# Causal scores in nine rounds for four groups instead of ten, and the order of all steps as a written list

## The chip, the cores and the metric

The kernel runs on one core of a Trainium2 chip. Its time is device microseconds of one execution; the median of three runs of the kernel before is 550.99 us (550.4 to 551.45). A profiled execution shows what each engine did: TensorE (PE: matmuls; PEld: its weight loads), VectorE (DVE), ScalarE (ACT), GpSimd (POOL), SyncE (SP, which issues most DMAs). Times in a profile count from the first instruction.

## The reference

Two layers, each an attention block A and a feed-forward block B, with residuals. There are 2048 tokens of width 640. A has 32 heads of 20; the tokens are cut into four segments of 512. Within a segment there is causal softmax attention; across segments a running memory M, z is read and then updated. The two results are mixed by a gate per head.

```python
q, k, v = heads(x @ wq), heads(x @ wk), heads(x @ wv)     # (32, 4 segments, 512, 20)
for s in range(4):
    p = softmax(q[s] @ k[s].T * 20 ** -0.5 + causal)       # 512 x 512 for each head
    a_dot = p @ v[s]
    a_mem = (phi(q[s]) @ M) / (phi(q[s]) @ z + 1e-6)       # phi(t) = t + 1 if t > 0 else exp(t)
    o[s] = sigmoid(beta) * a_mem + (1 - sigmoid(beta)) * a_dot
    M, z = M + phi(k[s]).T @ v[s], z + sum(phi(k[s]))
x = x + merge(o) @ wo
x = x + relu(layernorm(x) @ w1) @ w2                       # 640 -> 1728 -> 640
```

The input of A is layernorm(x) too. All of it is done twice with the same weights.

## The kernel before

One core keeps all weights and x in its memory. The eight pairs of layer and segment go through projections, scores, memory, output projection and feed-forward, and the phases of neighbouring segments overlap.

*Groups, pairs, rounds.* A group is four heads of one segment; there are 64 groups in the two layers, taken in 32 pairs (index m; z is 0 or 1 within a pair). Queries and keys of a pair lie in a padded buffer `pad`, four heads at partitions 0, 32, 64 and 96, twenty rows each; there are four such buffers, filled by SP's DMAs from a scratch tensor in device memory (`fill`). Keys are cut into four blocks j of 128. For block j only queries from 128j on are computed: 512, 384, 256 and 128 columns. `ROUNDS` packs these, for two groups, into five rounds of 512 columns: (z=0, j=0); (z=0, j=1 and 3); (j=2 of both); (z=1, j=0); (z=1, j=1 and 3). A round is issued by `scores` (matmuls at L1301). The four heads of a round use four tiles of 32 by 128 of the array side by side. It writes two slots X and Y of two PSUM banks each, and both must be free.

*Exponentials, masks, apply.* `exps` (L1365) empties each slot with one ScalarE instruction of 128 lanes by 1024 elements into the probability buffer `PT`, of which there is one for z=0 and one for z=1. `causal` (L1377) sets what lies over the diagonal to zero with GpSimd, four masks a group. `apply` (L1397) multiplies the probabilities of a group with its values: 16 matmuls on four tiles of 128 by 32, one for each head; the result lies in one of four single PSUM banks `MISC`, and is evicted to `otu` (L1407). Groups 6 and 7 of the first segment go another way (L1436).

*Everything else.* Projections, feed-forward, memory and transposes (helper lines L774 and L777) also write the four `MISC` banks. L774 issues a matmul on the whole 128 by 128 array, L777 the same work as four matmuls on tiles of 128 by 32. Which form is taken is chosen when a step is placed (`either`). PSUM is evicted by ScalarE or VectorE (`evac`).

*What sets the order.* Each phase is a generator that yields steps with the tokens they wait for. `Sched.run` places one step at a time: of the steps that are ready to be placed it takes the one with the earliest start by its own estimates, corrected by priorities, by allowances for late inputs (`SOFT`, `SOFT_DMA`, `LONE_NS`, `COLS_LAG`), and by a table `SHIFT` of offsets. The result is one fixed instruction sequence for each engine, with semaphores between them; nothing is decided on the chip.

Of the kernel before, what the change touches and what calls it, by code (L numbers as in the profile page):

```python
# [5 lines left out]
dt = mybir.dt  # L6
# [27 lines left out]
PTH = 1280  # L34
BY_TOKEN = range(6,8)
PT_OFF = [0, 512, 1024, 896]
# [73 lines left out]
class Op:  # L110

    def __init__(self, alts, waits, dma=None, acq=None, urgent=False, take=(), mode="full", lag=0.0, port=False):
        self.lag = lag
# [8 lines left out]
        self.urgent = urgent  # L125
        self.take = take
        self.data = 0.0
# [32 lines left out]
class Spawn:  # L160
    def __init__(self, prio, gen):
        self.prio = prio
        self.gen = gen


LONE_NS = 300.0
SWITCH_NS = 96.0
COLS_LAG = 1500.0
SOFT = 400
SOFT_DMA = 1000  # L170
SOFT_FROM = ("sc",6,4,1)
SEM_NS = 60.0
PE_MARGIN = 80.0
HOLDERS = 1
SHIFT = {
# [41 lines left out]
}  # L217
HOLD_TOL = {"pe": 220.0, "act": 150.0, "dve": 200.0, "pool": 0.0, "sp": 0.0}


class Sched:


    def __init__(self, prog):
        self.P = prog
        self.free = {e: 800.0 for e in ENGS}
        self.t = {}
        self.events = {}
        self.streams = []
        self.dma_free = 0.0  # L230
        self.rank = {}
        self.mode = "full"
        self.soon = 0.0
        self.landed = set()
        self.met = {}
        self.seen = {}
        self.phase = {}
        self.made = {}
        self.held = {"dve": [], "pool": []}

    def add(self, prio, gen):
        self.streams.append([prio, gen, None, None, False])
        self.rank[id(gen)] = 0
# [8 lines left out]
    def enter(self, gen, phase):  # L252
        if self.phase.get(id(gen)) != phase:
            self.phase[id(gen)] = phase
            self.made[id(gen)] = 0

    def place(self, n, gen):
        k = self.made.get(id(gen), 0)
        return n, self.phase.get(id(gen), 0), sum(k >= x for x in (6, 20, 60))

# [6 lines left out]
    def _fill(self, st):  # L267
        while st[2] is None and not st[4]:
            try:
                y = next(st[1]) if st[3] is None else st[1].send(st[3][0])  # L270
            except StopIteration:
                st[4] = True
                return
            st[3] = None
            st[2] = y

    def _settle(self, st):

        while True:
            self._fill(st)  # L280
            if st[4]:
                return False
            y = st[2]
            if isinstance(y, (Op, Either)):
                return True
            if isinstance(y, Spawn):
                self.add(y.prio, y.gen)
                self.rank[id(y.gen)] = self.rank[id(st[1])]
                st[2], st[3] = None, (None,)
            elif isinstance(y, Need):  # L290
                if y.key not in self.events:
                    return False
                st[2], st[3] = None, (self.events[y.key],)
            else:
                s = self._pick(y.slots)
                if s is None:
                    return False
                s.free = False
                st[2], st[3] = None, (s,)
# [5 lines left out]
    def _mode(self, op):  # L305
        if op.cols is None:
            return op.mode
# [1437 lines left out]
```

## Time and profile before

| | value |
|---|---|
| median of the runs | 550.99 us |
| profiled execution, first to last instruction | 549.3 us |
| TensorE busy | 539.8 us, 98% |
| VectorE busy | 427.8 us, 78% |
| ScalarE busy | 406.0 us, 74% |
| GpSimd busy | 195.7 us, 36% |
| exponentials L1365 | 320, 308.9 us |
| score matmuls L1301 | 1024 |

"Busy" is the union of the instructions' times. Matmuls are pipelined: one of 512 columns lasts 379 ns in the rows, though the next can start long before that. The time that a matmul takes from the stream is therefore read from start to start in the timeline. A row of a group has the line, the engine, the operation, output and input, the shape, the count, then busy time and mean nanoseconds of one, then the idle time ahead of it and what ended that. A row of the timeline has the start, the length, the engine, the line and the count of merged instructions. In a row of stretches stand the bounds, the length, then busy time for PE, PEld, DVE, ACT and POOL, the granted clock, the DMA share and GB/s.

### The profile page before, as it was taken

How to read it: one execution, taken by the hardware profiler on the slowest of the kernel's cores; microseconds unless marked ns; L12 is line 12 of the kernel's file. 1: busy time of each engine (PE TensorE's matmuls, PEld its weight loads, DVE VectorE, ACT ScalarE, POOL GpSimd, SP SyncE). 2: the span in 40 equal slices, each digit the busy share in tenths (PEclk: the TensorE clock that was granted, in tenths of full speed). 3: DMA queues.
4: the chain of work that ended last, by engine and by line, in shares of the span. 5: the costliest groups of instructions: out<-in, count | busy, mean ns of one | idle time of the engine just before them, and what ended most of it. 6: DMA issues, size and time to landing. Idle time of an engine off the chain costs nothing.

```text
span 549.3 us, 20483 instructions
## 1 busy us (share of the span) xinstructions
PE 539.8 (98%) x9025; PEld 305.5 (56%) x9025; DVE 427.8 (78%) x1067; ACT 406.0 (74%) x516; POOL 195.7 (36%) x305
## 2 busy tenths in 40 slices
PE   7999999999999999999999999999999999999997
PEld 6543464455554546646556555564646654757656
DVE  4899999898999989898778858997899788417102
ACT  5699899789888987788888867897778787350130
POOL 5255444333453334443433423433333333201000
PEclk9999999999999999999999999999999999999999
DMA  8699979715384175438384743336246511541201
GB/s 270 165 198 253 245 158 223 221 44 116 89 165 98 40 180 77 75 68 120 47 212 93 116 116 93 58 69 104 50 139 130 117 32 22 106 63 33 71 2 51
DMA packets 133325, 62.20 MB, mean 113 GB/s; under 512 B 112116, under 2 KB 123124, under 8 KB 133236
## 3 DMA queue, kind: packets, MB, share of 16 engines
q1 hardware_dynamic: 132672, 60.36, 51.5%
q8 instruction: 71, 1.16, 0.9%
q10 hardware_dynamic: 564, 0.53, 0.4%
q14 instruction: 18, 0.15, 0.1%
HBM read 20.56 MB, written 12.85 MB: 61 GB/s over the span
## 4 chain that ended last, share of the span: by engine, by line
PE 88%; ACT 6%; DVE 2%; DMA 2%; SPq 1%; issue 0%
PE ps L774 35%; PE ps L777 35%; PE ps L1301 8%; PE ps L1397 6%; ACT PT L1365 5%; PE ps L1180 2%; DMA x_sb<-in_A_x_dram 1%; PE ps L1572 1%; PE ps L1238 1%; DMA pad<-scr 1%; SPq L602 1%; DVE xn_tok L841 0%; SPq L612 0%; DVE stats L795 0%; DVE x_sb L1614 0%; DVE o_sb L1491 0%
## 5 line engine op out<-in xcount | busy, mean ns | idle before, releaser
L1365 ACT ACTIVATE PT<-ps 128x1024 bf16<-128x1024 f32 x320 | 308.9, 1028 | 59.3 <-PE ps L1301 57.6
L1377 POOL TENSOR_SCALAR_AFFINE_SELECT PT<-PT 128x512 bf16<-128x512 bf16 x256 | 169.3, 679 | 241.1 <-ACT PT L1365 241.0
L777 PE MATMUL ps<-xnT,w_r 128*32 128x512 bf16 x1256 | 76.0, 379 | 0.0
L777 PE MATMUL ps<-w_r,hT 128*32 128x320 bf16 (+1 forms) x1764 | 67.8, 295 | 0.0
L1614 DVE TENSOR_TENSOR x_sb<-x_sb,ps 128x320 bf16<-128x320 bf16 (+1 forms) x65 | 30.7, 474 | 43.6 <-PE ps L777 38.7
L1301 PE MATMUL ps<-pad 20*128 20x512 bf16 (+3 forms) x1024 | 63.4, 301 | 1.2 <-ACT PT L1365 0.7
L774 PE MATMUL ps<-w_r,hT 128*128 128x320 bf16 x404 | 64.2, 300 | 0.0
L795 DVE BATCH_NORM_STATS2 stats<-x_sb 128x6 f32<-128x320 bf16 x124 | 55.0, 478 | 3.8 <-DMA x_sb<-in_A_x_dram 3.0
L777 PEld LDWEIGHTS ps<-w_r,hT 128*32 128x32 bf16 x1764 | 45.2, 97 | 12.6 <-issue 1.4
L1595 ACT ACTIVATE hT<-ps 128x512 bf16<-128x512 f32 x50 | 29.9, 599 | 29.0 <-PE ps L777 25.6
L774 PE MATMUL ps<-xnT,w_r 128*128 128x512 bf16 x206 | 50.8, 380 | 0.0
L774 PEld LDWEIGHTS ps<-w_r,hT 128*128 128x128 bf16 x404 | 37.6, 98 | 19.4 <-issue 4.9
L1301 PEld LDWEIGHTS ps<-pad 20*128 20x128 bf16 x1024 | 17.9, 92 | 52.9 <-issue 24.5
L777 PEld LDWEIGHTS ps<-xnT,w_r 128*32 128x32 bf16 x1256 | 31.6, 97 | 27.8 <-issue 2.0
L1519 DVE TENSOR_TENSOR x_sb<-x_sb,ps 128x320 bf16<-128x320 bf16 x64 | 29.7, 478 | 20.4 <-PE ps L777 16.0
L811 POOL TENSOR_TENSOR rstd<-lnU,mhalf 128x2 f32<-128x2 f32 (+2 forms) x27 | 21.1, 782 | 63.5 <-DVE lnU L807 60.4
L1407 DVE CAST otu<-ps 128x512 bf16<-128x512 f32 x52 | 35.6, 685 | 9.1 <-PE ps L1397 8.2
L1397 PE MATMUL ps<-PT,v_aug 128*21 128x128 bf16 (+3 forms) x896 | 40.3, 300 | 0.0
L1594 DVE TENSOR_SCALAR hT<-ps 128x512 bf16<-128x512 f32 x54 | 36.5, 681 | 1.7 <-PE ps L774 0.7
L1491 DVE TENSOR_TENSOR o_sb<-otk,rden 128x320 bf16<-128x320 bf16 x62 | 34.8, 588 | 0.5
L981 DVE CAST stg<-ps 128x512 bf16<-128x512 f32 (+1 forms) x37 | 24.7, 669 | 12.5 <-PE ps L774 6.3
L1146 ACT ACTIVATE stg<-stg 128x512 bf16<-128x512 bf16 x50 | 31.7, 635 | 2.0 <-DVE rtmp L1144 1.8
(118 smaller groups left out, 731.5 us busy)
## 6 DMA issues: line engine op xcount, KB each, us to landing
pad<-scr SPq DMA_DIRECT2D x124, 80.0 KB
scr<-stg SPq DMA_DIRECT2D x34, 256.0 KB, 2.5
out_dram<-x_sb SPq DMA_DIRECT2D x15, 160.0 KB, 1.9
w_r<-in_B_w_dram SPq DMA_DIRECT2D x10, 216.0 KB, 4.0
w_r<-in_B_w_dram SPq DMA_DIRECT2D x13, 160.0 KB, 2.8
x_sb<-in_A_x_dram SPq DMA_DIRECT2D x10, 160.0 KB, 3.2
scr<-w_r SPq DMA_DIRECT2D x5, 256.0 KB, 4.2
wv_r<-in_A_wv_dram SPq DMA_DIRECT2D x1, 800.0 KB, 9.7
```

What stands on the lines that cost most here:

```text
L774: return e.matmul(view(dst.ap, b), a, b, start=(k == 0), stop=(k == last))
L777: return e.matmul(view(dst.ap[rows], b), part, b, start=(k == 0), stop=(k == last))
L795: tk = yield dve(320, 1, lambda e, c2=c2: e.bn_stats(stats6[:, t, c2, :], x_sb[:, t, c2 * 320:(c2 + 1) * 320]), xt)
L1146: te = yield act(512, lambda e, q=q: e.activation(q, q, ACT.Exp), [tr] + p, psum=False)
L1301: fns.append([(lambda e, z=z, j=j, hh=hh, N=N, o=o, sl=sl, q=hh % 2: e.matmul(slot.ap[:, q, o:o + N], sl.ap[32 * hh:32 * hh + DH, z, 0, 12 ...
L1365: tx = yield act(1024, lambda e, dst=dst, src=src: e.activation(dst, src, ACT.Exp, scale=SCALE), sc + pw)
L1377: tm = yield pool(600.0, lambda e, reg=reg: e.affine_select(out=reg, in_=reg, pattern=[[0, 4], [1, 128]], compare_op=ALU.is_ge, fill=0.0, ...
L1397: fns.append((lambda e, OD, j=j, hh=hh: e.matmul(OD.ap[32 * hh:32 * hh + DH + 1, 128 * j:L], VAUG[vx(a, s)][:, j, 4 * g + hh, :], pt.ap[:, ...
L1407: te = yield evac(L, 1, lambda e: e.tensor_copy(dst, OD.ap), lambda e: e.activation(dst, OD.ap, ACT.Copy), [tk] + OTU[0].tks)
L1491: to = yield dve(320, 1, lambda e, z=z, dst=dst: e.tensor_tensor(dst, av[:, z, :, :, 0:DH], rd.ap[:, z].to_broadcast([128, NJ, 4, DH]), AL ...
L1594: th = yield evac(512, 1, lambda e: e.tensor_scalar(hT[:, dc, :], bk.ap[:, :], 0.0, None, ALU.max), lambda e: e.activation(hT[:, dc, :], b ...
L1614: ta = yield dve(n, 1, lambda e: e.tensor_tensor(x_sb[:, t, c0:c0 + n], x_sb[:, t, c0:c0 + n], bk.ap[:, 0:n], ALU.add), [tk], urgent=True)
```

## The change

*Scores.* For a layer's first segment (`plain(m)`) the five rounds stay. In the other three segments a group's blocks are cut along the diagonal. What is left of the full blocks, without one square of 64 by 64 for each key block, fills two rounds of 512 columns for each group (`FULLS`: 448+64, and 192+256+64 columns). The squares left out, four for each of four heads in four groups (two pairs), make one further round (`DIAG`): 64 matmuls of 64 columns on eight tiles of 32 by 64 of the array, which write lanes 0 to 63 and 64 to 127 separately. It stands behind the second round of every second pair and reads the padded buffers of both pairs. So four groups take nine rounds instead of ten.

*Behind it.* The squares go to a new buffer `DG`, the rest to a shorter `PT` (1024 columns instead of 1280 for a head). A slot of the diagonal round is emptied by two ScalarE instructions of 64 lanes by 1024 elements. The masks are four a group as before, in other places: two on `PT`, both behind the second of its two rounds, and two on `DG`. `apply` takes nine pieces a head instead of four in these segments: 36 matmuls. At the start of these segments in each layer VectorE zeroes a part of `DG`. There are three padded buffers instead of four.

*Tokens.* In every second tile of 128 tokens the two halves of 64 are exchanged in memory, so that the squares of odd key blocks lie in the upper lanes; x is loaded, and the result stored, by DMAs of 64 partitions and two tiles. The last tile's store is split into halves on the queues of SP and ScalarE.

*Order.* The rules, priorities, allowances and the table are gone. A list `ORDER` names, step by step, which generator gives the next step (its number in the order of `S.add`; 40 more for one that it spawned; 80 more for the second form: VectorE instead of ScalarE for an eviction, quarter-width tiles instead of full ones for a matmul group). There are 7192 quarter-width matmuls of L777's kind instead of 4604, and 712 full ones of L774's kind instead of 1359. TensorE changes its tile shape 308 times instead of 322. ScalarE gets 17 more instructions; VectorE has 17 copies fewer.

```diff
-PTH = 1280
+PTH = 1024
-PT_OFF = [0, 512, 1024, 896]
+PT_OFF = [0, 512, None, 896]
+FULLS = (((0, 64, 448), (3, 384, 64)), ((2, 320, 192), (1, 256, 256), (1, 128, 64)))
+DIAG = ((0, 0, 0), (0, 3, 448), (1, 2, 256), (1, 1, 192))
+SUMS = ((0, 0, 448, 64), (3, 448, 64, 384), (2, 512, 192, 320), (1, 704, 256, 256), (1, 960, 64, 128))
-SOFT = 400
-SOFT_DMA = 1000
-SHIFT = {
...
+ORDER = """
+36 37 35 21 36 37*3 36*2 35 21 36 21*2 37 21 26 21*2 22 35 37 26*4 21 22*3 21*2 108 28*3 37 26 23 28 23 148 28 37*6
...
+    def run(self):
+        for word in ORDER.split():
+            code, _, count = word.partition("*")
+            for _ in range(int(count or 1)):
+                n, other = int(code) % 80, int(code) >= 80
+                st = tops[n] if n < 40 else next(x for x in self.kids[id(tops[n - 40])] if not x[3])
+                self._record(st, st[1].fn() if isinstance(st[1], Either) else st[1], other)
...
-        NPAD, NXT, NXN, NPT = 4, 2, 2, 2
+        NPAD, NXT, NXN, NPT = 3, 2, 2, 2
+        DG = sb("DG", [128, 2, 4, 4 * 128])
...
+        def plain(m):
+            return m % (NSEG * G // 2) < G // 2
+        def rounds(m):
+            return [u for u in range(5) if plain(m) or u != 2 or m % 2 == 0]
+        def turn_of(m, u):
+            if plain(m):
+                return [(z, 0, 128 * j, 128, 128 * j, L - 128 * j, o) for z, j, o in ROUNDS[u]]
+            if u == 2:
+                return [(z, 64 * (j % 2), q0, 64, q0, 64, 128 * z + 64 * y) for z in range(4) for y, j, q0 in DIAG]
...
-                        slot.ap[:, q, o:o + N], sl.ap[32 * hh:32 * hh + DH, z, 0, 128 * j:128 * j + 128],
-                        sl.ap[32 * hh:32 * hh + DH, z, 1, 128 * j:L]),
+                        slot.ap[p:p + nk, q, o:o + nq], sl.ap[32 * hh:32 * hh + DH, z, 0, k0:k0 + nk],
+                        sl.ap[32 * hh:32 * hh + DH, z, 1, q0:q0 + nq]),
...
+                            moves = [(DG[r, t].rearrange("p z (h x) -> p h z x", h=4)[:, hs],
+                                      bkp.ap[r].rearrange("p h (z x) -> p h z x", z=4)) for t, r in enumerate(SIDES)]
...
+                sums = [(j, lambda hh, c0=c0, nq=nq: pt.ap[:, hh, c0:c0 + nq], q0, nq) for j, c0, nq, q0 in SUMS]
+                sums += [(j, lambda hh, j=j, y=y: DG[:, j % 2, n % 4, 128 * hh + 64 * y:128 * hh + 64 * y + 64], q0, 64)
+                         for y, j, q0 in DIAG]
```

More of the change, by code (lines that the diff above doesn't have):

```diff
@@ L110, with __init__ @@
 class Op:
-    def __init__(self, alts, waits, dma=None, acq=None, urgent=False, take=(), mode="full", lag=0.0, port=False):
-        self.lag = lag
+    def __init__(self, alts, waits, dma=None, acq=None, take=(), mode="full", port=False):
         self.port = port
@@ L454, in pe, with _times @@
-def pe(ns, fns, waits=(), acq=None, take=(), mode="full", lag=0.0):
-    return Op([("pe", ns, fns, 190.0)], waits, acq=acq, take=take, mode=mode, lag=lag)
+    def _times(self, op, k, waits):
+        e, hold, fns, tail = op.alts[k]
+        m = PE_MARGIN if e == "pe" else 0.0
+        if e == "pe" and op.mode == "cols" and op.cols_ns is not None:
+            hold = op.cols_ns
+        if e == "pe" and op.mode != self.mode:
+            hold = hold + SWITCH_NS
+        start = max([self.at(t) + SEM_NS + m for t in waits], default=0.0)
+        start = max(self.free[e], start)
+        if e == "dve" and op.port:
+            for a, b in self.held["pool"][-6:]:
+                if a <= start + 66.0 < b:
+                    hold = max(hold, b - start + op.data - 70.0)
+        if e == "pool":
+            for a, b in self.held["dve"][-6:]:
+                if a < start + hold and b > start:
+                    hold = hold + b - max(a, start)
+        return start, start + hold
@@ new lines, in run @@
+    def run(self):
+        tops = list(self.streams)
+        first = tops[0]
+        self._settle_all()
+        for word in ORDER.split():
[4 more added lines that the diff above has]
+                self._record(st, st[1].fn() if isinstance(st[1], Either) else st[1], other)
+                self._settle(st)
+                self._settle_all()
+                if isinstance(first[1], Either):
+                    first[1].fn()
+        assert not self.streams
@@ new lines, in _record @@
+    def _record(self, st, op, other):
+        k = int(other and len(op.alts) > 1)
+        e, _, fns, tail = op.alts[k]
+        if op.cols is not None:
+            op.mode = "cols" if other else "full"
+            fns = op.cols if other else fns
+        waits, slot = op.waits, None
+        for s in op.take:
+            s.free = False
+        if op.acq is not None:
+            slot = self._pick(op.acq)
+            slot.free = False
+            waits = waits + slot.tks
+            fns = [(lambda eng, fn=fn, slot=slot: fn(eng, slot), mark) for fn, mark in fns]
+        start, end = self._times(op, k, waits)
+        self.P.waits(e, waits)
+        self.free[e] = end
+        if e == "pe":
+            self.mode = op.mode
+        if e == "dve" and op.port:
+            self.held[e].append((end - op.data, end))
+        elif e == "pool":
+            self.held[e].append((start, end))
+        if op.dma is not None:
+            tk = self.P.dma(e, fns[0][0], op.dma)
+            self.dma_free = max(self.dma_free, start + 300.0) + tail[1]
+            self.t[(id(tk[0]), tk[1])] = max(self.dma_free, end) + tail[0]
+            if tail[2]:
+                self.free[e] = max(end, self.dma_free)
+            out = tk
+        else:
+            marks = []
+            for fn, mark in fns:
+                tk = self.P.op(e, fn, mark)
+                if tk is not None:
+                    self.t[(id(tk[0]), tk[1])] = end + tail
+                    marks.append(tk)
+            out = marks[0] if len(marks) == 1 else (marks or None)
+        st[1], st[2] = None, ((slot, out) if slot is not None else out,)
@@ L458, in either, with pe @@
+def pe(ns, fns, waits=(), acq=None, take=(), mode="full"):
+    return Op([("pe", ns, fns, 190.0)], waits, acq=acq, take=take, mode=mode)
 def either(op, cols, ns=None):
@@ L1371, in causal, with flat, mask @@
+        def flat(m):
+            b = 2 * (m % 2)
+            return DG[:, :, b:b + 2].rearrange("p t z (y q) -> p t (z y) q", y=2)
+        MK = {}
         def causal(m):
+            def mask(reg, n, base, w):
+                return pool(600.0, lambda e: e.affine_select(
+                    out=reg, in_=reg, pattern=[[0, reg.shape[1]], [1, n]], compare_op=ALU.is_ge, fill=0.0, base=base,
+                    channel_multiplier=-1), w)
             mk = [[], []]
-            for u, parts in enumerate(ROUNDS):
+            last = []
+            for u in rounds(m):
@@ new lines, in items @@
+        def items(f, count):
+            for n in range(count):
+                yield from f(n)
+        S.add(scores())
+        S.add(exps())
+        S.add(items(causal, NSEG * G))
+        S.add(items(apply, 2 * NSEG * G))
+        S.add(each(free_v))
+        S.add(items(turn_pair, NSEG * G))
+        S.add(items(divide, NSEG * G))
+        S.add(each(turn_o))
+        S.add(each(out_proj(0)))
+        S.add(each(out_proj(1)))
+        S.add(each(ln_b(0)))
+        S.add(each(ln_b(1)))
+        S.add(each(fill))
@@ L1712, in bass_interleave_layers__memory_aug_infini_attn__dense_activation_relu__prompt_kernel @@
+        S.add(each(proj_v))
+        S.add(each(ffn))
+        S.add(each(ffn_rest))
+        S.add(each(store))
+        S.add(warm_pe())
+        S.add(consts())
+        S.add(loads())
+        S.add(late_loads())
         S.run()
```

667 lines of the change are left out of this document (326 added, 341 removed), and 41 rows, old and new, of the table SHIFT.

## The prediction

> **What bounds the kernel now.** I read the page first (shares, slices, chain), then the stretches, then the waits, then the timeline around single rounds of scores.
>
> ```profile
> span 549.3 us, 20483 instructions
> PE 539.8 (98%) x9025; PEld 305.5 (56%) x9025; DVE 427.8 (78%) x1067; ACT 406.0 (74%) x516; POOL 195.7 (36%) x305
> ...
> PEclk9999999999999999999999999999999999999999
> ...
> PE 88%; ACT 6%; DVE 2%; DMA 2%; SPq 1%; issue 0%
> ...
> L1365 ACT ACTIVATE PT<-ps 128x1024 bf16<-128x1024 f32 x320 | 308.9, 1028 | 59.3 <-PE ps L1301 57.6
> L1377 POOL TENSOR_SCALAR_AFFINE_SELECT PT<-PT 128x512 bf16<-128x512 bf16 x256 | 169.3, 679 | 241.1 <-ACT PT L1365 241.0
> ```
>
> TensorE is busy 98% at the full granted clock and carries 88% of the chain. Busy is not peak, so what counts is whether TensorE ever runs out of work. By stretches (length, then busy time of PE, PEld, DVE, ACT, POOL):
>
> ```profile
> 13.70:50.00 36.30, 35.00 (x412) 16.55 (x414) 33.73 (x88) 31.13 (x41) 16.78 (x25) 1.00 0.87 190
> 50.00:150.00 100.00, 98.78 (x1389) 52.29 (x1381) 92.15 (x229) 87.55 (x109) 41.96 (x64) 1.00 0.71 166
> 250.00:350.00 100.00, 100.00 (x1648) 55.49 (x1644) 77.73 (x191) 81.94 (x103) 38.77 (x58) 1.00 0.54 108
> 490.00:549.30 59.30, 56.28 (x1500) 38.93 (x1492) 16.70 (x43) 11.73 (x20) 1.39 (x2) 1.00 0.14 37
> ```
>
> Between 250 and 350 us TensorE has no idle time; what it loses before 150 us is small. A second engine is close behind: ScalarE. One period of the middle stage shows the lockstep:
>
> ```profile
> 236.82 0.40 PE L1301 MATMUL ps<-pad 20*128 20x256 bf16 x8
> 237.15 2.56 PE L777 MATMUL ps<-xnT,w_r 128*32 128x512 bf16 x44
> 237.25 1.94 ACT L1365 ACTIVATE PT<-ps 128x1024 bf16<-128x1024 f32 x2 [0.47 <-PE ps L1301]
> 239.08 0.63 ACT L1146 ACTIVATE stg<-stg 128x512 bf16<-128x512 bf16 x1
> 239.64 0.39 PE L1301 MATMUL ps<-pad 20*128 20x512 bf16 x4
> 239.97 0.83 PE L777 MATMUL ps<-xnT,w_r 128*32 128x512 bf16 x12
> 240.07 1.94 ACT L1365 ACTIVATE PT<-ps 128x1024 bf16<-128x1024 f32 x2 [0.36 <-PE ps L1301]
> ```
>
> A round of scores (L1301) fills two double PSUM banks; two exponentials empty them in 1.94 us; the next round needs both. From one round to the next 2.82 us pass (236.82 to 239.64), and TensorE fills them with 44 projection matmuls. Rounds cannot follow faster than the exponentials allow. The tightest I find is this:
>
> ```profile
> 147.57 0.39 PE L1301 MATMUL ps<-pad 20*128 20x512 bf16 x4
> ...
> 148.00 1.94 ACT L1365 ACTIVATE PT<-ps 128x1024 bf16<-128x1024 f32 x2 [0.66 <-PE ps L1301]
> ...
> 150.04 0.40 PE L1301 MATMUL ps<-pad 20*128 20x384 bf16 x8
> ```
>
> 0.43 us to the first exponential, 1.94 for two, 0.10 back: 2.47 us. So in the middle TensorE is the limit with about 0.3 us of slack to ScalarE per round, and any saving must come out of TensorE's stream without pulling rounds below 2.47 us.
>
> **The change, part by part.** The profiled execution took 549.3 us from first to last instruction; the median of the runs is 551.0, so 1.7 us lie around it. The sum is made on 549.3.
>
> *Fewer rounds.* Three segments of four, in both layers, hold 24 pairs of groups. Ten rounds per four groups become nine: 160 rounds become 148. One round costs TensorE what lies between its first matmul and the next instruction, 0.33 us (239.64 to 239.97), and the entry before it. For the entry I need the column rate:
>
> ```profile
> 60.78 1.24 PE L774 MATMUL ps<-hT,wk_r 128*128 128x512 bf16 x5
> 61.86 0.43 PE L774 MATMUL ps<-wv_r,hT 128*128 128x320 bf16 x2
> ```
>
> Five full matmuls of 512 columns take 1.08 us, 0.216 each. The 44 quarter-width ones at 237.15 are eleven such steps, 2.38 us, but the next round starts after 2.49: entry 0.11. Of the 0.33, 0.216 are columns, so leaving costs 0.11 too. Twelve rounds at 0.44 us: -5.3.
>
> *Other mode changes.* By the order of the instructions TensorE changes tile shape 322 times before and 308 times after. The missing rounds take 24 away, so ten are added elsewhere: +1.0 at about 0.10. The rest of the shift from full to quarter-width matmuls (1359 to 712 full ones of L774's kind) costs nothing: 0.216 per 512 columns in both forms above.
>
> *Shorter pieces inside ordinary rounds.* Rounds of 384+128 and 256+256 columns take 0.33 like one of 512 (236.82 to 237.15), so 448+64 and 192+256+64 are costed at nothing beyond it; if each further step cost as in the next rows it would be under 1 us over 96 rounds.
>
> *The diagonal round.* Twelve rounds consist of 64 matmuls of 64 columns on eight tiles of 32x64. No such tile is in the trace. Nearest are short matmuls on four tiles:
>
> ```profile
> 250.98 0.35 PE L1238 MATMUL ps<-v_aug,phk 128*32 128x42 bf16 x24
> 251.15 0.72 PE L1572 MATMUL ps<-xnT,w_r 128*32 128x256 bf16 x19
> ```
>
> 24 matmuls of 42 or 63 columns in 0.17 us: 7.1 ns each, 28 ns per step of four. If eight tiles go through a step as four do, the round's eight steps take 0.23 us, as its columns do (0.216): 0. If the 7.1 ns hold per matmul, 64 take 0.45: +0.24 a round, +2.9 in all. Since the four row tiles of a normal round add nothing, I stay near the lower end, +0.04 a round: +0.5. Range 0 to +2.9.
>
> *Applying the probabilities.* 48 groups go from 16 to 36 matmuls with the same 1280 columns.
>
> ```profile
> 296.00 0.66 PE L1238 MATMUL ps<-v_aug,phk 128*32 128x147 bf16 x48
> 296.54 0.72 PE L1397 MATMUL ps<-PT,v_aug 128*21 128x512 bf16 x16
> 297.08 1.27 PE L777 MATMUL ps<-w_r,hT 128*32 128x320 bf16 x32
> ```
>
> From 296.54 to 297.08, 0.54 us, is 1280 columns at the same rate, so steps of 128 and more are free. The 24 short ones above lie 0.04 us over their columns (1218 columns on four tiles, 0.13 us), 7 ns a step. Five more steps: 0 to 0.035 us an apply, 0 to +1.7 in all; I take the middle, +0.9.
>
> *ScalarE.* Its evictions, for what follows:
>
> ```profile
> L1595 ACT ACTIVATE hT<-ps 128x512 bf16<-128x512 f32 x50 | 29.9, 599 | 29.0 <-PE ps L777 25.6
> ...
> L1036 ACT ACTIVATE v_aug<-ps 128x320 bf16<-128x320 f32 x16 | 7.0, 446 | 0.6 <-PE ps L774 0.4
> ```
>
> 320 exponentials stay 320: 272 as before, 48 of 64 lanes by 1024 elements. By elements per lane they cost the same 1.03; if lanes counted, 0.60 as a 128x512 eviction does, 20 us off an engine that is not the bound; no row has a dearer one. After a diagonal round four of them must end: 0.43 + three at 0.92 (1.94 less 1.02) + 1.02 + 0.10 = 4.3 us. Priced by the rows above, the new order puts 4.85 to 7.2 us of TensorE work behind each of the twelve. Hidden; each exponential may be 0.13 us dearer before TensorE waits. Another 17 PSUM evictions move from VectorE to ScalarE, some 9 us, mostly in the gaps of 0.36 and 0.47 shown above.
>
> *Masks, memory, DMAs.* 256 masks of 679 ns stay; a group's first mask now waits for two rounds, but GpSimd idles 241 us behind L1365 and the order puts the apply 7 to 9 us after the last score instead of 4 to 6. Two VectorE memsets of 64x1024 are new, about 1 us each, hidden (without cover 2 us). Padded buffers go from four to three, and a diagonal round needs two at once: a reload still has about 16 us before its first reader, six rounds at 2.8. Loads and stores of x move the same bytes in other pieces: 0, or 0.2 us at the last store.
>
> Sum: -5.3 + 1.0 + 0.5 + 0.9 = -2.9, from -4.3 to +0.3. That makes 546.4 profiled and 548.1 as a run.
>
> [...]
>
> **The rivals.**
>
> *Waits at the start go too (faster still).* The order is now free where a rule chose before, and TensorE has waits before 70 us:
>
> ```profile
> 17.31 1.04 PE L774 MATMUL ps<-xnT,wq_r 128*128 128x512 bf16 x4 [0.44 <-DVE w_r L1036]
> 34.45 0.85 PE L774 MATMUL ps<-wv_r,hT 128*128 128x320 bf16 x5 [0.32 <-DVE v_aug L1036]
> 56.43 0.82 PE L774 MATMUL ps<-hT,wq_r 128*128 128x512 bf16 x3 [0.52 <-DVE otu L1407]
> 65.24 0.39 PE L1301 MATMUL ps<-pad 20*128 20x512 bf16 x4 [0.43 <-DMA pad<-scr]
> ```
>
> With the smaller ones the lost starts sum to about 4 us after 16 us; three quarters gone gives 545. Against it: the first-segment rounds are as dense as before (14 or 15 of them under 2 us apart), so ScalarE is as far behind there.
>
> *The gain is given back by ScalarE (no change).* A probability buffer is overwritten only after its apply. In the new order the apply stands a median of 1.5 us ahead of the round whose exponentials overwrite it, before 4.8, and six stand behind that round. Where that delays the pair of exponentials, the next round slips and the 0.3 us of slack is used up; 0.23 us on 12 quads, three times each, takes back 2.8: 550.8. For it: rounds are 2.55 to 2.75 us apart in most of the list, near 2.47.
>
> *Bank reuse is too tight (slower).* Four single PSUM banks serve everything but scores. A 512-column eviction holds one for 0.2 us of draining (0.43 less 0.216), its own 0.60 and 0.10 back. That is 0.9 us, or 0.75 for 320 columns. Priced by the rows above, 10 of 493 reuses had under 0.2 us to spare before, 72 of 495 after; eleven have none. If an eviction is queued behind an exponential (0.92), each such reuse costs TensorE up to 0.1 us or so: 72 x 0.07 = 5, net +2.1, 553. It turns the sign at 0.04 us on each of the 72. For it: the counts. Against: reuses with 0.1 spare did not stop TensorE before.
>
> *A floor per matmul, tiles or not.* At 11 ns (48 matmuls in 0.54 us, 296.00 to 296.54, long ones among them) a diagonal round takes 0.72, +0.5 each, and an apply +0.22: +6 + 10.6, net 564. The pure short row speaks against it.
>
> **How the numbers follow.** The sum stands: 0.42, 546.7 to 551.0 by its bounds with 548.1 likeliest. Start waits gone: 0.16, 545. Given back: 0.18, about 550.8. Tight banks: 0.19, 553. Floor: 0.05, 564. A measurement here tells 0.2%, 1.1 us, from no change. Faster: nine tenths of the first and the second, 0.54. Same: the rest of the first and the third, 0.22. Slower: 0.24. The range leaves out the floor, the far side of the tight banks and the lowest of the start waits: 544.6 to 553.2; the likeliest case alone 546.7 to 551.0.
>
> **What would show it.** Right: 148 rounds; the time from a diagonal round's first matmul to the next instruction 0.33 to 0.40; an apply of 36 matmuls 0.54 to 0.57; 64-lane exponentials at 1.03; TensorE without idle time between 100 and 480 us. Wrong: diagonal rounds near 0.6, or exponentials over 1.16 with TensorE waiting behind them; waits of PE on evictions (L1036, L1407, L1595 by their new lines) that sum to over 2 us after 70 us; a wait for padded buffers on one DMA queue.

## The result and the profile after

The changed kernel takes 564.8 us (median of 4 runs, 563.47 to 565.77), the kernel before 550.97 (550.4 to 551.45): the ratio is 1.0249, 95% interval 1.0233 to 1.0265. It is slower by 13.8 us, where 2.9 less were forecast. The profiled executions differ by 11.8 us (spans of 561.1 and 549.3); that of the changed kernel is the fastest of its four (563.47).

The page of the changed kernel, first its span, busy times, packets of instructions and the shares of the chain of waits:

```profile
span 561.1 us, 28721 instructions
...
PE 544.4 (97%) x13135; PEld 329.0 (59%) x13135; DVE 410.1 (73%) x1052; ACT 413.7 (74%) x533; POOL 196.3 (35%) x305
...
q8 instruction: 103, 1.69, 1.3%
...
PE 77%; DVE 8%; DMA 6%; ACT 5%; issue 1%; SPq 1%; POOL 1%; DVEq 0%
```

The same line on packets in the page of the kernel before:

```profile
q8 instruction: 71, 1.16, 0.9%
```

TensorE has lost share of the chain (88% to 77%) to VectorE and DMAs, and 13135 matmuls have come to it in 103 packets instead of 9025 in 71. From 70 us to the end, first the kernel before, then the changed one (length; then busy time and count of PE, PEld, DVE, ACT, POOL):

```profile
70.00:561.00 491.00, 475.47 (x8247) 270.39 (x8244) 368.58 (x913) 349.48 (x435) 162.82 (x243) 1.00 0.46 94
```

```profile
70.00:561.00 491.00, 479.64 (x12143) 293.49 (x12141) 354.54 (x904) 354.64 (x447) 165.33 (x245) 1.00 0.52 99
```

The kernel before ends at 549.3 and has been busy for 475.47 of its 479.3 us; the changed one has been busy for 479.64 of 491. So the loss is mostly standing time. To sort it I compared each matmul's start with the time at which its tile of the array was free, counted delays over 40 ns, and put each down to the last semaphore that its group waited for, or to none. All sums of standing below are made in this way. The labels stand for the runs that are told in the next section.

| kernel | run, us | matmuls | packets | before 70 us | after 70: no semaphore | VectorE | DMA | ScalarE, GpSimd | after 70, all |
|---|---|---|---|---|---|---|---|---|---|
| before | 551.0 | 9025 | 71 | 8.9 | 0 | 0.4 | 0 | 0.8 | 1.2 |
| changed | 564.8 | 13135 | 103 | 7.7 | 5.7 | 4.1 | 3.8 | 0.6 | 14.3 |
| both forms split, in before | 598.4 | 13629 | 106 | 8.2 | 38.8 | 0.4 | 2.3 | 1.5 | 43.0 |
| 512 columns split, in before | 554.6 | 10829 | 85 | 8.5 | 1.3 | 0.4 | 1.3 | 0.7 | 3.7 |
| changed, full form where free | 557.2 | 10066 | 79 | 8.8 | 0.2 | 2.7 | 3.5 | 0.5 | 6.9 |
| changed, steps moved | 565.2 | 13135 | 103 | 7.2 | 5.7 | 4.1 | 5.3 | 0.7 | 15.8 |

The waits of TensorE as the profile lists them (total, times, longest), in the changed kernel:

```profile
PE ps L776 <- issue: 2.1, 6, 0.6
PE ps L1234 <- issue: 1.4, 1, 1.4
...
PE ps L776 <- DMA w_r<-in_B_w_dram: 0.9, 1, 0.9
...
PE ps L776 <- DMA xnT<-xn_tok: 0.7, 1, 0.7
PE ps L776 <- DVE hT L1678: 0.6, 1, 0.6
...
PE ps L1176 <- DVE om_sb L1191: 0.6, 1, 0.6
```

"issue" is a wait for nothing that the profile shows. In the list of the kernel before, no row names it, and the longest rows are

```profile
PE ps L735 <- DVE warm L678: 1.1, 1, 1.1
PE ps L866 <- DVE xn_tok L853: 1.1, 2, 0.6
PE ps L1301 <- ACT PT L1365: 0.7, 2, 0.5
```

of which the first two lie before 70 us.

In time, examples of each kind in the changed kernel (start, length, then what TensorE waited for):

```profile
157.12 0.19 PE L1234 MATMUL ps<-v_aug,phk 128*32 128x42 bf16 x3
158.74 0.24 PE L1234 MATMUL ps<-v_aug,phk 128*32 128x63 bf16 x9 [1.43 <-issue]
...
170.92 0.35 PE L1176 MATMUL ps<-BD,phs 128*32 128x147 bf16 x12 [0.55 <-DVE om_sb L1191]
...
453.05 1.26 PE L776 MATMUL ps<-xnT,w_r 128*32 128x512 bf16 x20 [0.66 <-DMA xnT<-xn_tok]
```

At 158.74 TensorE stops for 1.6 us in the middle of twelve matmuls of one step, with nothing to wait for that the profile shows (1.43 us of "issue").

Of the rounds themselves, a diagonal one, and an apply of 36 matmuls with the ordinary round behind it:

```profile
300.03 0.71 PE L1316 MATMUL ps<-pad 20*64 20x64 bf16 x64
300.67 0.46 PE L776 MATMUL ps<-w_r,hT 128*32 128x320 bf16 x8
```

```profile
171.75 0.61 PE L1480 MATMUL ps<-PT,v_aug 128*21 128x448 bf16 x20
172.19 0.29 PE L1480 MATMUL ps<-DG,v_aug 128*21 128x64 bf16 x16
172.30 0.60 PE L776 MATMUL ps<-xnT,w_r 128*32 128x512 bf16 x8
172.84 0.40 PE L1316 MATMUL ps<-pad 20*128 20x448 bf16 x8
173.17 0.25 PE L1176 MATMUL ps<-BD,phs 128*32 128x147 bf16 x4
```

The diagonal round takes 0.64 us (300.03 to 300.67), the apply 0.55 (171.75 to 172.30), the round of 448+64 columns 0.33 (172.84 to 173.17).

So three losses stand in the trace: diagonal rounds (3.7 us), stops without a semaphore (5.7), and waits on VectorE and DMAs (7.5 more than before). The experiments take them one by one.

### The profile page after: what moved, and what is told of

Its sections match the earlier page's. It is cut to its first block, busy times and chain, and to the rows that moved or that the text cites. A ratio compares the mean times of both kernels' runs of the same rounds, so it can differ in the third digit from the quotient of the medians.

```text
span 561.1 us, 28721 instructions
## 1 busy us (share of the span) xinstructions
PE 544.4 (97%) x13135; PEld 329.0 (59%) x13135; DVE 410.1 (73%) x1052; ACT 413.7 (74%) x533; POOL 196.3 (35%) x305
## 4 chain that ended last, share of the span: by engine, by line
PE 77%; DVE 8%; DMA 6%; ACT 5%; issue 1%; SPq 1%; POOL 1%; DVEq 0%
PE ps L776 48%; PE ps L773 14%; PE ps L1316 8%; PE ps L1480 5%; ACT PT L1396 3%; DMA xnT<-xn_tok 2%; DMA otk<-otu 2%; DVE xn_tok L840 2%; DVE stats L794 1%; DMA x_sb<-in_A_x_dram 1%; PE ps L1176 1%; ACT DG L1396 1%; DVE x_sb L1603 1%; DMA phk<-phs 1%; DVE o_sb L1575 1%
## 5 line engine op out<-in xcount | busy, mean ns | idle before, releaser
L1396 ACT ACTIVATE PT<-ps 128x1024 bf16<-128x1024 f32 x256 | 248.9, 1035 | 42.7 <-PE ps L1316 40.5
L1415 POOL TENSOR_SCALAR_AFFINE_SELECT PT<-PT 128x512 bf16<-128x512 bf16 (+1 forms) x144 | 96.8, 693 | 180.2 <-ACT PT L1396 180.0
L776 PE MATMUL ps<-xnT,w_r 128*32 128x512 bf16 x1740 | 115.8, 380 | 1.5 <-DMA xnT<-xn_tok 0.7
L776 PE MATMUL ps<-w_r,hT 128*32 128x320 bf16 x2496 | 111.1, 299 | 1.3 <-DMA w_r<-in_B_w_dram 0.9
L1415 POOL TENSOR_SCALAR_AFFINE_SELECT DG<-DG 128x512 bf16<-128x512 bf16 x112 | 73.0, 688 | 53.9 <-ACT DG L1396 53.9
L1396 ACT ACTIVATE DG<-ps 64x1024 bf16<-64x1024 f32 (+1 forms) x64 | 64.9, 1035 | 10.4 <-PE ps L1316 9.4
L1316 PE MATMUL ps<-pad 20*64 20x64 bf16 (+5 forms) x1984 | 62.9, 238 | 1.0 <-issue 0.4
L776 PE MATMUL ps<-wo_r,oT 128*32 128x320 bf16 x808 | 46.9, 300 | 0.9 <-issue 0.9
L776 PE MATMUL ps<-wv_r,xnT 128*32 128x320 bf16 x752 | 44.8, 300 | 0.6 <-DVE hT L1678 0.6
L776 PE MATMUL ps<-xnT,wq_r 128*32 128x512 bf16 x484 | 40.3, 380 | 0.5 <-issue 0.5
```

Of the source, the lines that this page charges most:

```text
L776: return e.matmul(view(dst.ap[rows], b), part, b, start=(k == 0), stop=(k == last))
L1316: fns.append([(lambda e, z=z % 2, p=p, k0=k0, nk=nk, q0=q0, nq=nq, o=o, hh=hh, sl=pads[m + z // 2], q=hh % 2: e.matmul(slot.ap[p:p + nk, q ...
L1396: tx = yield act(1024 if len(moves) == 1 else 1180, lambda e, dst=dst, src=src: e.activation(dst, src, ACT.Exp, scale=SCALE), sc + pw)
L1415: return pool(600.0, lambda e: e.affine_select(out=reg, in_=reg, pattern=[[0, reg.shape[1]], [1, n]], compare_op=ALU.is_ge, fill=0.0, base ...
```

## The experiments

### What a diagonal round is bound by

```diff
-                return [(z, 64 * (j % 2), q0, 64, q0, 64, 128 * z + 64 * y) for z in range(4) for y, j, q0 in DIAG]
+                return [(z, 64 * (j % 2), q0, 64, q0, 32, 128 * z + 64 * y) for z in range(4) for y, j, q0 in DIAG]
```

> The changed kernel with 32 instead of 64 columns in each of the 64 matmuls of a diagonal round; half of those scores is left out. Everything else, the list too, is the same. In the changed kernel a diagonal round lasts 0.636 us from its first matmul to the next instruction. If each pair of weight load and matmul costs its 8.2 ns whatever it moves: 0.636 again, and the run stays within 1 us of 564.8. If the columns are the price (523 ns for 64 x 64 columns over the 0.113 us of entering and leaving): 0.37 us, run near 561.6. If a tile loads and then moves, 65 ns for a turn of eight of which the columns are 27: 0.53 us, run near 563.5.

It ran in 565.93 us (563.31 to 570.28), no faster than the changed kernel. The round, in the timeline:

```profile
299.72 0.68 PE L1316 MATMUL ps<-pad 20*64 20x32 bf16 x64
300.33 1.40 PE L776 MATMUL ps<-w_r,hT 128*32 128x320 bf16 x34
```

0.61 us with half the columns: the columns are not the price, and a tile that loads and then moves in series is excluded too (0.53). The single starts in the trace of the changed kernel say how the 0.64 come about: at 300.03 the first 32 matmuls start within 0.14 us, in bursts of eight 3 to 4 ns apart; the second burst starts 53 ns after the first, the others some 31 ns apart, little over what 64 columns take (27 ns, at 0.216 us for 512). Then nothing starts for 0.10 us, and the other 32 start 8.3 ns apart one by one. In ten of the twelve rounds the longest gap, 0.08 to 0.10 us, stands ahead of the 33rd matmul in this way. In one round of this experiment three matmuls start, then nothing for 0.15 us, then a burst of 32 across the border of the two sets, and the rest again at 8.3 ns. So it isn't the second set of squares that is slow: in these rounds some 32 pairs of weight load and matmul go out at once after a pause, in 0.14 us, and beyond them pairs come every 8.3 ns. Why it is some 32, and why the next pairs come at 8.3 ns, isn't shown.

### Stops without a semaphore: packets of instructions

The sharpest test makes TensorE's stream in the kernel before as dense in instructions as the changed one's and denser, and leaves the order and the other engines' work alone. `quarter` in `group` gets a half `h`, and each quarter-width matmul becomes two:

```diff
-                def quarter(e, dst, rows, part, k=k, b=b):
-                    return e.matmul(view(dst.ap[rows], b), part, b, start=(k == 0), stop=(k == last))
+                def quarter(e, dst, rows, part, h, k=k, b=b):
+                    if len(b.shape) == 2:
+                        w = n // 2
+                        return e.matmul(dst.ap[rows][:, w * h:w * h + w], part, b[:, w * h:w * h + w],
+                                        start=(k == 0 and h == 0), stop=True, skip_group_check=True)
...
-                            for c, (rows, part) in enumerate(quarters(a))]
+                            for h in range(2) for c, (rows, part) in enumerate(quarters(a))]
```

> The kernel before, with each quarter-width matmul of the projections and the feed-forward (128x32 tiles) done as two of half the columns, in the same order; 13629 matmuls instead of 9025, the same columns, mode switches and work on the other engines. A step of four such matmuls costs 2 to 2.4 ns above its columns, so 1150 more steps cost 2.5 to 2.8 us. Theory dense instructions: the packets of instructions rise from 71 to about 107 as in the changed kernel, TensorE's waits without a semaphore (1.4 us in all of the kernel before after its start, 5.7 after 70 us in the changed kernel) rise to 4 to 7 us, run near 559. Theory order (the waits come from the written list): such waits stay under 1.5 us after 70 us, run near 553.7.

598.42 us, ratio 1.0885 (1.0852 to 1.0919). The direction is the one that packets give, the size is far above what I expected: 38.8 us of stops. The further steps themselves account for little of the 48 us: in the kernel before, quarter-width steps of 512 and 320 columns start 216 and 136 ns apart (medians), which makes 0.417 ns a column and 2.7 ns a step, and 1150 further steps at that are 3 us, an estimate. Its waits, packets and a stretch of its timeline near the end:

```profile
PE ps L779 <- issue: 29.6, 24, 2.7
```

```profile
q8 instruction: 106, 1.74, 1.2%
```

```profile
571.57 1.98 PE L779 MATMUL ps<-w_r,hT 128*32 128x160 bf16 x104 [1.07 <-issue]
573.36 0.33 PE L779 MATMUL ps<-w_r,hR 128*32 128x160 bf16 x8
573.50 0.46 PE L779 MATMUL ps<-w_r,hT 128*32 128x160 bf16 x16
575.31 1.71 PE L779 MATMUL ps<-w_r,hT 128*32 128x160 bf16 x88 [1.35 <-issue]
576.83 0.33 PE L779 MATMUL ps<-w_r,hR 128*32 128x160 bf16 x8
576.97 0.74 PE L779 MATMUL ps<-w_r,hT 128*32 128x160 bf16 x32
578.78 1.43 PE L779 MATMUL ps<-w_r,hT 128*32 128x160 bf16 x72 [1.07 <-issue]
```

From stop to stop stand 104 + 8 + 16 and 88 + 8 + 32 matmuls: 128 each time. A packet is 16 KB (1.74 MB in 106). TensorE's queue holds 18186 instructions in the kernel before and 26414 in the changed one, for 71 and 103 packets: 256 to a packet, which is 128 pairs at 64 bytes an instruction. The packets arrive all through the run, in the changed kernel from 13.7 to 550.3 us. From stop to stop 3.74 and 3.47 us pass. On the instruction queue itself the closest starts of two packets lie 3.26 to 3.65 us apart, according to the kernel (3.65 in the kernel before, 3.31 in the changed one): about 1.0 us of transfer and 2.3 to 2.6 us from its end to the next start. So in these stretches TensorE gets a pair per 27 ns (3.47 us by 128) and hardly more. A step of four matmuls of 160 columns takes 69 ns (the 104 from 571.57 to 573.36 take 1.79 us), 17 ns a pair: where that lasts here, TensorE stops for 1.07 to 1.35 us in each 3.5 or so.

The place of the stops in the stream says the same. Count weight loads, matmuls and semaphore instructions along TensorE's queue, 256 to a packet. After 70 us the changed kernel has twelve delays over 0.1 us that stand 192 or 193 instructions past a multiple of 256, 6.5 us together; the run above has 36, 40.4 us; the kernel before has none. In the changed kernel every such delay without a semaphore stands there, and the long waits for VectorE and DMAs stand elsewhere. Two of the twelve, at 325.79 (0.54 us, in the middle of a step of four) and 377.03 (0.29), are in the table under VectorE and DMA, because their groups had waited for a semaphore earlier; by place they are stops, which makes 6.5, 3.6 and 3.5 us of the changed kernel's 5.7, 4.1 and 3.8.

If that is so, splitting only where a pair still lasts 27 ns should cost next to nothing (the change against the edit above):

```diff
+                H = 2 if n == 512 else 1
...
-                        w = n // 2
+                        w = n // H
```

> The kernel before with only the quarter-width matmuls of 512 columns split in two, not those of 320: 10829 matmuls. Eight matmuls of 256 columns take 0.22 us, 27 ns a pair, just what one packet per 3.45 us supplies; those of 320 columns take 33 ns a pair as before. Theory packets: little or no standing, waits without a semaphore after 70 us under 4 us (38.8 with both split), 451 more steps at 2 to 2.4 ns cost 1 us, run 552 to 556. If standing grew with the number of matmuls and not with their density: two fifths of the 38.8 us, run near 568.

554.59 us, ratio 1.0079 (1.0059 to 1.01), 1.3 us of stops. So density decided here, not the number of matmuls: 1804 further ones brought 1.3 us of stops, the 4604 of the run above 38.8.

Now the other way round: density taken out of the changed kernel. 951 steps of the list lie in stretches with rounds of scores on both sides, where the full form costs no further change of tile shape; they are marked in the list and issued in the full form:

```diff
-                n, other = int(code) % 80, int(code) >= 80
+                n, other, whole = int(code) % 80, int(code) >= 80, int(code) >= 400
...
-            fns = op.cols if other else fns
+            fns = op.cols if other and not whole else fns
```

> The changed kernel with the same list, but wherever a stretch of quarter-width matmuls has rounds of scores on both of its ends, it is issued in the full 128x128 form: no more changes of tile shape (301 instead of 308), 10066 matmuls instead of 13135, 1.6 us more columns in the memory steps, and about 3 us more for the 951 full matmuls. Theory packets (one packet of 16 KB holds 128 pairs of weight load and matmul, and two packets never start within 3.3 us, so that TensorE stands without a semaphore where it uses pairs faster than one per 27 ns): packets fall from 103 to about 79, waits without a semaphore after 70 us from 5.7 to under 2 us, run about 562, between 560 and 564. If those waits have another cause: they stay at 5 to 6 us, and the run is 566 to 568.

557.15 us, ratio 1.0121 (1.0102 to 1.014): 7.6 us off the changed kernel, more than expected. The profiled executions differ by 5.5 us (555.6 and 561.1), the one the slowest of its four runs and the other the fastest; the stops fall from 5.7 to 0.2. The 3 us set down for the 951 full matmuls were an estimate that no trace shows: in the kernel before, steps of 512 and of 320 columns start 216 and 136 ns apart (medians) in the full form as in quarter width. Its packets, and the place of the longest stop, which has gone but for 0.2 us one step earlier:

```profile
q8 instruction: 79, 1.29, 1.0%
```

```profile
156.28 0.31 PE L776 MATMUL ps<-wv_r,xnT 128*32 128x320 bf16 x4
156.41 0.26 PE L1234 MATMUL ps<-v_aug,phk 128*32 128x42 bf16 x12
```

### Is the diagonal round's price on the path?

In that better kernel I left out half of the diagonal's matmuls:

```diff
-... for z in range(4) for y, j, q0 in DIAG]
+... for z in range(4) for y, j, q0 in DIAG if y == 0]
```

> The changed kernel in the full form where that is free (557.15 us), with 32 instead of 64 matmuls in each of the twelve diagonal rounds; the other half of their squares is left out. Theory price per pair on TensorE's path: 32 pairs at 7.8 to 8.2 ns and 0.113 us of entering and leaving make a round of 0.36 to 0.38 us instead of 0.636, and TensorE is late by 3.1 to 3.3 us less at the end: run near 554. If the longer diagonal rounds are covered by waits that come behind them anyway: the rounds shorten as much, but the run stays above 556.

552.27 us (550.91 to 553.69), 4.9 less. The round:

```profile
293.56 0.33 PE L1316 MATMUL ps<-pad 20*64 20x64 bf16 x32
293.82 1.94 PE L773 MATMUL ps<-w_r,hT 128*128 128x320 bf16 x13
```

0.26 us, not the 0.37 expected: the 32 matmuls go out as the first 32 of a whole round did. The second 32 cost 0.37 us (0.64 less 0.26), twelve times 4.5 us, and the run gives all of it back (4.9). So the price is on TensorE's path; what was wrong in this expectation is a price per pair from the first pair on.

### Waits on VectorE and DMAs

First by moving what waited. Steps of other generators were pulled ahead of a step that had stood still, fifteen in all (the expectation miscounts them as thirteen); the list is otherwise the same. Here is the place at 170.9 us, where 112 is the feed-forward and 97 the reading of the memory:

```diff
-2 17 97 112 2 1 6 1 17 112*2 72 27 17 83 112 97 112 0
+2 17 112*5 97 2 1 6 1 17 72 27 17 83 97 0
```

> The changed kernel with thirteen TensorE steps of the list pulled forward past a step that waited in the trace, at 170.9, 196.4, 268.0, 309.4, 325.8 (VectorE evictions) and 453.1 us (transposes); nothing else is moved. Theory local margins (the list has put single steps too close behind their evictions, and VectorE is not behind as a whole): these six waits, 3.6 us in all, shrink by about 2 us and none of that size comes in their place; run about 562.8. Theory engines behind (VectorE or the transposes are late by queues that the steps' places don't touch): the waits return within some microseconds, run 564 to 566.

565.21 us (561.38 to 567.81): no gain. In the timeline the step of 170.92 starts without a wait, and the next of its kind waits:

```profile
171.76 0.34 PE L1175 MATMUL ps<-BD,phs 128*32 128x147 bf16 x12
...
173.19 0.35 PE L1175 MATMUL ps<-BD,phs 128*32 128x147 bf16 x12 [0.21 <-DVE om_sb L1190]
```

VectorE's sum stays at 4.1 us, and the waits on DMAs rise to 5.3, with one of 2.06 us on a transpose at 388.98 where the changed kernel's profiled execution has no stop. Transposes of `xnT` take 1.26 to 2.33 us in the changed kernel. "Local margins" falls.

The run with half the columns has the list as it was, so its trace shows what comes again. TensorE waits for VectorE at the same places (there 77.5, 88.0, 170.2, 196.2 and 308.9 us), but the wait of 1.1 us for weights at 111.9 is gone, and one of 0.8 us for another transpose (`oT`), at 265.1, is new. So in these two executions the longer waits on VectorE come again with the list, and some of those on DMAs don't.

Both edits together:

> Both edits together: the thirteen steps moved and the full form wherever it adds no change of tile shape. If both theories hold, about 560; if only packets, 562; if neither, 567. Faster than the kernel before (551) by no theory.

558.16 us, ratio 1.0136 (1.0112 to 1.016): the gain of the full form alone. What was expected if both held, 560, is met by one of them with more than its share.

Then by the order. The rules of the kernel before (its `Sched` without the table `SHIFT`) were given the new rounds, and as a control the old ones:

```diff
-class Sched: ...          (walks ORDER)
+class Sched: ...          (the rules of the kernel before, SHIFT = {})
```

> The new rounds, applies, masks and stores of the changed kernel, but the order made by the rules of the kernel before, without its table of shifts; to be read against the old rounds under the same rules. By columns, changes of tile shape and the measured 0.636 us of a diagonal round the new rounds cost TensorE 0.4 us more there. Theory order: both runs wait alike, the difference between them is within 3 us, and this run has few waits without a semaphore (10543 matmuls) and no more waits on transposes than the other. Theory rounds (the new rounds, applies and buffers themselves stop TensorE): this run is 8 us or more above the old rounds under the same rules, with TensorE waiting on exponentials, masks or probability buffers.

> The kernel before, without its table of shifts: old rounds, order by the rules alone. It is the control of the new rounds under the same rules. Theory order: within 3 us of them, both slower than the kernel before by what the table was worth, 5 to 15 us. Theory rounds: 8 us or more faster than the new rounds under the same rules.

574.78 us (ratio 1.0426, 1.039 to 1.0462) with the new rounds, 563.0 (1.0229, 1.02 to 1.0259) with the old ones: 11.8 us apart, with 14.9 and 10.0 us of standing after 70 us, 15.3 and 11.1 before. The longest of their waits, new rounds first:

```profile
PE ps L1296 <- ACT DG L1378: 2.8, 2, 2.3
PE ps L1296 <- ACT PT L1378: 2.4, 5, 1.2
PE ps L1462 <- POOL DG L1397: 2.3, 2, 1.2
```

```profile
PE ps L1260 <- ACT PT L1324: 4.7, 4, 2.0
PE ps L733 <- DVE otu L1366: 2.3, 2, 2.0
```

By the numbers set beforehand (8 us or more) this speaks for "rounds": rounds wait for the exponentials of the diagonal buffer and applies for its masks. But it isn't shown that the rounds cost those 8 us. 4.2 of the 11.8 are standing before 70 us, ahead of the first diagonal round (87 us). And around its longest waits TensorE was granted half its clock (0.50), with the new rounds for 13.7 us (120.5 to 130.7 and 181.9 to 185.3), with the old ones for 6.8 (93.3 to 100.1). Both orders are poor in places of their own, too. So the new rounds also got a table of shifts chosen for them, with the diagonal round at 0.56 us:

```diff
-SHIFT = {}
+SHIFT = {...}             (chosen for the new rounds)
-                    return pe(256.0 if on else 233.0, fns, a[1] + b[1] + a[0].tks + b[0].tks, take=[a[0], b[0]],
+                    return pe(560.0 if on else 233.0, fns, a[1] + b[1] + a[0].tks + b[0].tks, take=[a[0], b[0]],
```

> The new rounds, applies, masks and stores under the rules of the kernel before, with the diagonal round entered at 0.56 us and a table of shifts chosen anew for them; no written list. 10816 matmuls and 299 changes of tile shape; by columns, changes, diagonal rounds and applies TensorE's own work is 0.3 us more than in the kernel before. Theory order (the list, by packets and by margins, makes the loss): few waits without a semaphore (under 3 us after 70 us), all waits after 70 us under 8 us instead of 14.3, run 552 to 557. Theory rounds (the new rounds stop TensorE in any order): over 11 us of waits after 70 us, run 560 or more. By neither is it faster than the kernel before by more than 0.2%.

563.77 us, ratio 1.0218 (1.0176 to 1.0259), 12.2 us of standing after 70 us: by its numbers again "rounds", though 3.3 us of them are stops at the same place of a packet as above (1.8 at 109.77, 1.1 at 374.85). Its waits:

```profile
PE ps L1378 <- ACT PT L1460: 4.0, 6, 1.4
...
PE ps L838 <- DVE otu L1555: 1.4, 2, 1.0
```

In this kernel rounds wait for exponentials mostly between 90 and 161 us, in the list's they hardly do (0.3 us after 70). The list, the list with the full form, the rules and the rules with a table thus lose 14.3, 6.9, 14.9 and 12.2 us after 70 us, and by different releasers; none comes near the 1.2 of the kernel before. Under the same rules the new rounds stand 4.9 us longer than the old ones after 70 us; that no order of them can be free of waits isn't shown. What remains open is how the 7 us or so of waits on VectorE and DMAs divide between the list and the rounds.

No kernel here beats the kernel before. By columns, changes of tile shape, diagonal rounds and applies, the changed stream is TensorE's work of before to within half a microsecond (-5.3 + 1.0 + 3.7 + 0.3), so an order as free of waits as before would have won next to nothing.

## Why the prediction was wrong

- *Fewer rounds, -5.3; tile changes, +1.0.* 148 rounds are there, ordinary ones take 0.33 as before. These terms can't be read singly from the trace, but the whole closes: with the diagonal rounds and applies below -0.3 of stream, +13.1 of standing after 70 us and -1.2 before it make 11.6, against 11.8 of the spans. The sum's upper bound is 551.3 (551.0 and +0.3), not 551.0; nothing hangs on it.
- *The diagonal round, +0.5.* This step failed. It was said to go like four row tiles, 0.33 to 0.40; it took 0.64, +3.7 in all, more than the upper end of +2.9. The short row has 24 pairs, fewer than the 32 that go out at once, so it could not show what comes beyond them; the two readings of its 7.1 ns were 0 and +2.9 us, and the one at which a round costs nothing was taken. The 64 pairs cost 0.52 us (0.64 less 0.11 of entering and leaving), more than either reading gave (0.23 and 0.45).
- *Applying the probabilities, +0.9.* 0.55 us instead of 0.54: about +0.3. The mechanism (little above the columns) held, the size was off by 0.6.
- *From full to quarter-width matmuls "costs nothing".* This step failed, and it is the one that the runs settle. By columns it is true (0.216 us per 512 in both forms); but the 2588 further quarter-width matmuls, with 1728 short ones, brought 32 further packets, and where they lay dense TensorE stopped, 5.7 us by the table and 6.5 by place. No row of the kernel before showed such a stop, and I didn't read the line of the instruction queue. The runs with split matmuls (+48 us) and with the full form (-7.6) show it.
- *ScalarE.* 64-lane exponentials cost about what those of 128 lanes do (1018 and 1035 ns), as said:

```profile
L1396 ACT ACTIVATE PT<-ps 128x1024 bf16<-128x1024 f32 x256 | 248.9, 1035 | 42.7 <-PE ps L1316 40.5 <-PE ps L1480 1.1
L1396 ACT ACTIVATE DG<-ps 64x1024 bf16<-64x1024 f32 x48 | 48.9, 1018 | 8.8 <-PE ps L1316 7.9
```

  In the list's order TensorE hardly waits for them, so "the gain is given back by ScalarE" didn't happen.
- *Masks, evictions and DMAs "hidden".* This step failed too, by 7.5 us: 4.1 on VectorE, mostly its evictions, 3.8 on transposes and one load of weights, 0.4 before (6.7 without the two stops that stand in these columns). "Bank reuse is too tight" had the place: most of VectorE's 4.1 us are banks not yet emptied. It had the shape wrong: 13 waits of 0.04 to 0.72 us (one of them a stop by its place), not 72 of 0.07. Whether the list or the rounds bring these waits stays open. Transposes that take 1.26 or 2.33 us, and a list that waits for them at five places, I hadn't weighed.
- *Start waits.* 8.9 to 7.7 us: a small part of what that rival hoped for.
- *The rival at 564.* Its time came out by luck and its reason didn't: 11 ns per matmul would make a diagonal round 0.72 and an apply +0.22 us; they are 0.64 and +0.01.
- *Signs named.* Of those for "wrong", diagonal rounds near 0.6 came. Waits on VectorE's evictions after 70 us come to 1.9 us on the lines named there, and to 3.6 with those to `x_sb` and `om_sb`. The range left out what no row had a price for.

## What to carry to other kernels

Count instructions as well as columns: in these runs TensorE got one pair of weight load and matmul per 27 ns over stretches of several microseconds (3.47 us for 128), and one per 8.3 ns beyond the first 32 or so of a diagonal round. Here, splitting the work of the kernel before into narrower pieces brought 1.3 us of stops where a pair still lasted 27 ns, and 38.8 with pairs of 17 ns as well; the line of the instruction queue and waits put down to "issue" in the profile are where to look. And a saving of 5 us in a schedule with 1 us of standing has to be laid beside what the reordering may cost: here the changed kernel stands 13 us more after 70 us, more than twice what the rounds could save.

## What the hardware did that I had not expected

- In no kernel here did packets of instructions (16 KB, 128 pairs) start closer than 3.26 us (3.65 in the kernel before, 3.31 in the changed one); with both forms split, at 17 ns a pair, TensorE stood still 1.1 to 1.4 us in every 3.5 or so, 192 or 193 instructions past a multiple of 256.
- In the diagonal round at 300.03 of the changed kernel 32 pairs of 64 columns on eight tiles go out in 0.14 us; the 33rd comes 0.10 us later, and each further one after 8.3 ns. 32 matmuls make a round of 0.26 us, 64 one of 0.64.
- Behind a wait of 1.38 us the granted clock was 0.50. In the new rounds with their own table, ten full matmuls of 512 columns take 3.94 us behind that wait (92.67 to 96.61), 0.39 each instead of 0.216. The granted clock is 0.50 from 92.94 to 96.35, and again from 110.00 to 113.42 behind a stop of 1.8 us without a semaphore; over the 40 us around both it is 0.91:

```profile
92.33 0.40 PE L1378 MATMUL ps<-pad 20*128 20x192 bf16 x12 [1.38 <-ACT PT L1460]
92.67 4.02 PE L835 MATMUL ps<-xnT,w_r 128*128 128x512 bf16 x10
```

```profile
90.00:130.00 40.00, 35.68 (x692) 17.97 (x692) 29.99 (x71) 31.27 (x38) 13.88 (x21) 0.91 0.50 125
```

  Under the rules these stretches at half clock lasted 3.4, 6.8 and 10.2 us. The stop of 1.6 us at 158.74 in the changed kernel had no such effect (1.00 there), and what decides it isn't shown.
